# Scores of a windowed attention: keys and queries split into two float16 and multiplied on the two halves of the rows, in place of float32r keys stacked for each head

## The chip, the cores and the metric

The kernel runs on one core of a Trainium2 chip. The metric is the device time of one execution in microseconds, as a median of three runs. A profile of one execution gives the instructions of each engine: TensorE (PE, its weight loads as PEld), VectorE (DVE), ScalarE (ACT), GpSimd (POOL) and the DMA queue issued from SyncE (SP).

## The reference

Attention with four batches, eight heads, 768 positions and a head dimension of 64. Each position sees the first `n_sink` = 4 keys and the last `window` = 128 keys. The result (3072 tokens of width 512) goes through a feed-forward layer of width 2048 with an ELU between.

```python
scores = np.matmul(q, k.transpose(0, 1, 3, 2)) / np.sqrt(64)
rel = pos[:, None] - pos[None, :]
keep = (pos[None, :] < n_sink) | ((rel >= 0) & (rel < window))
a = softmax(np.where(keep, scores, -1e9))
x = np.matmul(a, v)                       # heads side by side: 3072 x 512
h = x @ w_in                              # 512 x 2048
g = np.where(h > 0, h, np.exp(np.minimum(h, 0)) - 1)
out = g @ w_out                           # 2048 x 512
```

Inputs are float32 and the output is float32. Precision beyond float16 is had by splitting a number into a float16 `hi` and a float16 rest `lo` and adding products: hi·hi + lo·hi + hi·lo.

## The kernel before

The 24 tiles of 128 tokens are grouped into nine chunks (`SIZES`: three of 2 tiles, six of 3). For a chunk, `attention(c)` goes over four pairs of heads and, in each pair, over the tiles. `feed_forward` then goes over the 16 slices of the hidden width (`NF`): twelve matmuls into `h` (L671), the ELU (L679 to L682), its split (`gh` on ACT, L684, and `gl` on POOL, L685), and 6 or 9 matmuls into `acc` (L692). The first two chunks take the feed-forward in two halves (`PARTS`), while the weights arrive: each of the 32 weight pieces comes as 64-bit words, is turned into float32 on ACT and DVE (L287 to L290), and is split into two float16 (ACT L436, POOL L437).

Attention of a tile and a pair of heads: scores for both heads into two banks `s`; mask and row minimum on DVE (L586), exponential on ACT (L588), normalised and split into float16 (ACT L600, DVE L601), transposed by a DMA (L619), multiplied with the split values on the two halves of the columns (`po`, L630 and L635), and moved out as `x` (L643, L644). A tile has keys of two tiles (264 columns with the sinks, `nb` = 2), or of one where it is the first tile of a batch (132 columns, `nb` = 1).

How the scores are made differs by chunk. In the first two chunks (`c < WHOLE`) the raw float32 keys and queries of a pair lie on the two halves of the 128 rows, 64 rows a head, and L567 multiplies them in float32. From the third chunk on (`c >= DUP`) each head has a block of its own, with its keys on both halves of the rows. `split_keys` loads it (L502), rounds keys and queries to float32r on ACT (L503), takes the rest of the keys on POOL (L507) and writes the rest of the queries over the lower half of the queries (L509, 64 rows). So one pass over 128 rows gives hi·hi + lo·hi: L560 multiplies by the keys' `hi`, L561 by their `lo`. These are two matmuls a head and four a pair, each with a float32r operand.

The order of work is written out ahead of time by a planner (`Plan`): tasks with modelled durations, a PE order by `pos`, list scheduling by due time on the other engines, and rings of buffers (`kq` = 3, `kqs` = 2, `s` = 2) as dependences. `keep_order` then fixes that order on each engine. At the end, `in_range` (L743) checks on DVE that sums, values and weights were within the limits of the split; its result decides whether `general_path` (a slow path, not run for these inputs) follows.

Of the kernel before, what the change touches and what calls it, by code (L numbers as in the profile page):

```python
# [9 lines left out]
F32 = mybir.dt.float32  # L10
# [35 lines left out]
LAG = 2  # L46
ROUNDS = 8
WHOLE = 2
DUP = 2
AHEAD = 5  # L50
V_AT = 7
V_AT0 = 5.0
# [3 lines left out]
def key_tiles(ch):  # L56

    return sorted({g for g in ch} | {g - 1 for g in ch if g % NT})
# [5 lines left out]
for _c, _ch in enumerate(CHUNKS):  # L64
    for _p in range(NP):
        V_OFF[_c, _p] = V_COLS
        V_COLS += (len(key_tiles(_ch)) + 1) * P
        for _e in range(2):
            KQ_OFF[_c, 2 * _p + _e] = KQ_COLS
            if _c >= DUP or _e:  # L70
                KQ_COLS += len(key_tiles(_ch)) * KW + len(_ch) * P
KQ_MAX = max(len(key_tiles(c)) * KW + len(c) * P for c in CHUNKS)
KL_MAX = max(len(key_tiles(c)) * KW for c in CHUNKS)
NK_MAX = max(len(key_tiles(c)) for c in CHUNKS)
TOK_MAX = max(SIZES) * P

# [267 lines left out]
def fast_path(tc, ctx, first, kq, vx, wt, out, nw, flag):  # L344
# [11 lines left out]

    kqs = first["kqs"]
    vs = first["vs"]
    kqr = rows("kq", [P, KQ_MAX + KL_MAX], F32R)
    vh = rows("vh", [P, (NK_MAX + 1) * P], F16, RINGS["vhl"])  # L360
    vl = rows("vl", [P, (NK_MAX + 1) * P], F16, RINGS["vhl"])
    vm = rows("vm", [P, NP, TOK_MAX], F32)
# [34 lines left out]

    nc1, nc2 = len(SIZES) * NF, len(SIZES) * NP  # L400
    checks = pool.tile([P, nc1 + nc2 + NW], F32, name="checks")
    es_of, v_top, w_top = checks[:, :nc1], checks[:, nc1 : nc1 + nc2], checks[:, nc1 + nc2 :]
    some = pool.tile([P, 4], F32, name="some")[:, 0:3]
    some16 = pool.tile([P, 4], BF16, name="some16")[:, 0:3]

# [66 lines left out]
    def attention(c):  # L472
# [14 lines left out]
        def split_keys(h):  # L487


            st = kqs[slot("kqs")]  # L490
            buf = kqr[slot("kq")] if c >= WHOLE else None
            o, kw = KQ_OFF[c, h], kc + qc
            if c < WHOLE:
                ld = None
                if (c, h) not in first["kq"]:
                    ld = add("SP", 0.4, lambda: nc.sync.dma_start(st[:, :kw], kq[:, o : o + kw]), lat=dma_us(P * kw * 4))
                users = []
                return st, None, ld, ld, users
            raw, hi = st[:, :kw], buf[:, :kw]
            ld = None  # L500
            if (c, h) not in first["kq"]:
                ld = add("SP", 0.4, lambda: nc.sync.dma_start(raw, kq[:, o : o + kw]), lat=dma_us(P * kw * 4))  # L502
            th = add("ACT", act_us(kw), lambda: nc.scalar.activation(hi, raw, AF.Copy), deps=[ld])  # L503

            def low():
                n = kc if c >= DUP else kw
                nc.gpsimd.tensor_tensor(buf[:, KQ_MAX : KQ_MAX + n] if c >= DUP else buf[:, kw : 2 * kw], raw[:, :n], hi[:, :n].bitcast(F32), ALU.subtract)  # L507
                if c >= DUP:
                    nc.gpsimd.tensor_tensor(hi[D:, kc:], raw[D:, kc:], hi[D:, kc:].bitcast(F32), ALU.subtract)  # L509

            tl = add("POOL", pool_us(kc) + pool_us(qc) if c >= DUP else pool_us(kw), low, deps=[th])
            users = []
            ring("kqs", [ld or th], [th, tl])
            ring("kq", [th], users)
            lo = buf[:, KQ_MAX : KQ_MAX + kc] if c >= DUP else buf[:, kw : 2 * kw]
            return hi, lo, th, tl, users

        k = 0
        for p in range(NP):
            kqp = [split_keys(2 * p + e) for e in range(2 if c >= DUP else 1)]  # L520


            st = vs[slot("vs")]
# [17 lines left out]
            for g in ts:  # L541
# [10 lines left out]
                pq = pqs[slot("pq")]  # L552
                pt = pts[slot("pt")]

                def scores(es_, sps=sps, qo=qo, c0=c0, wd=wd, kqp=kqp):
                    def run():
                        if c >= DUP:
                            hi, lo = kqp[es_[0]][:2]
                            sp, q = sps[es_[0]], hi[:, qo : qo + P]
                            nc.tensor.matmul(sp[:, :wd], q, hi[:, c0 : c0 + wd], start=True, stop=False)  # L560
                            nc.tensor.matmul(sp[:, :wd], q, lo[:, c0 : c0 + wd], start=False, stop=True)  # L561
                            return
                        hi, lo = kqp[0][:2]
                        if c < WHOLE:
                            for e in es_:
                                r = slice(e * D, (e + 1) * D)
                                nc.tensor.matmul(sps[e][:, :wd], hi[r, qo : qo + P], hi[r, c0 : c0 + wd], start=True, stop=True)  # L567
                            return
                        for n, (a, b) in enumerate(((hi, hi), (lo, hi), (hi, lo))):
                            for e in es_:  # L570
                                r = slice(e * D, (e + 1) * D)
                                nc.tensor.matmul(sps[e][:, :wd], a[r, qo : qo + P], b[r, c0 : c0 + wd], start=n == 0, stop=n == 2)
                    return run

                if c >= DUP:
                    scs = [add("PE", 0.22 if nb == 2 else 0.45, scores([e]), deps=kqp[e][2:4], pos=at[k] + 0.01 * e, line=1) for e in range(2)]
                else:
                    scs = [add("PE", 0.75, scores([0, 1]), deps=kqp[0][2:4], pos=at[k], line=1)] * 2
                for kk, sc_ in zip(kqp, scs):
                    kk[4].append(sc_)  # L580
                if c < WHOLE and j == 0:
                    ring("kqs", [kqp[0][2] or scs[0]], kqp[0][4])
                exps, st_users = [], []
                for e in range(2):
                    ee, me = e3[:, e, :wd], mn[:, e : e + 1]
# [155 lines left out]
        seen += new  # L741

    def in_range():  # L743
        for r, most in ((es_of, EXP_MAX), (v_top, V_MAX)):
            nc.vector.tensor_scalar(r, r, most, None, ALU.is_le)
        for i in range(2):
            nc.vector.tensor_reduce(some[:, 1 + i : 2 + i], w_top[:, i::2], AX.X, ALU.max)
        nc.vector.tensor_scalar(w_top, w_top, W_MAX, None, ALU.is_le)
        nc.vector.tensor_reduce(some[:, 0:1], checks, AX.X, ALU.min)
        nc.vector.tensor_scalar(some[:, 1:3], some[:, 1:3], W_MIN, float(P), ALU.is_ge, ALU.mult)  # L750
        nc.vector.tensor_copy(some16, some)
# [5 lines left out]
        nc.vector.tensor_tensor(flag, flag, some[:, 0:1], ALU.mult)  # L757

    sp = s_ps[slot("s")]
    a = add("DVE", 2.0, in_range, deps=seen + exps_done)  # L760
    b = add("PE", 0.1, lambda: nc.tensor.matmul(sp[:, 0:3], ones, some16, start=True, stop=True), deps=[a], pos=start + 2 * LAG - 1.5)
    ring("s", [b], [add("DVE", 0.6, decide, deps=[b])])
    for writer, users in later:
# [27 lines left out]
def general_path(tc, ctx, kq, vx, wt, out, nw):  # L791
# [50 lines left out]
    for b in range(B):  # L842
        x = sb.tile([P, ND, S], F32, name=f"g_x{b}", tag="g_x", bufs=1)
        for h in range(H):
# [3 lines left out]
            for c, ch in enumerate(CHUNKS):  # L848
                kts = key_tiles(ch)
                for i, g in enumerate(ch):  # L850
                    if g // NT != b:
                        continue
                    j, ts = kts.index(g), slice(g % NT * P, (g % NT + 1) * P)
                    o = KQ_OFF[c, h]
                    r = slice(0, D) if c >= DUP else slice(h % 2 * D, (h % 2 + 1) * D)
                    nc.sync.dma_start(kt[:, ts], kq[r, o + j * KW + NS : o + (j + 1) * KW])
                    o += len(kts) * KW + i * P
                    nc.sync.dma_start(qt[:, ts], kq[r, o : o + P])
                    o = V_OFF[c, h // 2] + j * P + (h % 2) * D
                    nc.sync.dma_start(vt[:, g % NT, :], vx[:, o : o + D])  # L860
# [47 lines left out]
def layouts(q, k, v):  # L908

    kT = k.transpose(0, 1, 3, 2).reshape(B, H, D, NT, P)
    kx = np.concatenate([np.broadcast_to(kT[:, :, :, :1, :NS], (B, H, D, NT, NS)), kT], axis=4)
    qT = q.transpose(0, 1, 3, 2).reshape(B, H, D, NT, P)
    kq = np.empty((P, KQ_COLS), q.dtype)
    vx = np.zeros((P, V_COLS), v.dtype)
    for c, ch in enumerate(CHUNKS):
        kts = key_tiles(ch)  # L920
        far = [g // NT for g in ch if g % NT >= 2]
        for h in range(H):
            e = h % 2
            o = KQ_OFF[c, h]
            for src, tiles in ((kx, kts), (qT, ch)):
                for g in tiles:
                    w = src.shape[4]
                    for r in (0, 1) if c >= DUP else (e,):
                        kq[r * D : (r + 1) * D, o : o + w] = src[g // NT, h, :, g % NT]
                    o += w  # L930
            o = V_OFF[c, h // 2] + e * D
            for g in kts:
                vx[:, o : o + D] = v[g // NT, h, g % NT * P : (g % NT + 1) * P]
                o += P
            if far:
                assert min(far) == max(far)
                for r in range(e * NS, 96, 32):
                    vx[r : r + NS, o : o + D] = v[far[0], h, :NS]
    return kq, vx
# [77 lines left out]
```

## Time and profile before

| | |
|---|---|
| median of 3 runs | 658.06 us (657.52 to 658.17) |
| the profiled execution | 658.03 us, its span 656.2 us (1.8 us lie around the span) |
| granted TensorE clock, mean | 0.984 |
| PE / PEld busy | 611.0 us (93%) / 370.1 us (56%) |
| DVE / ACT / POOL busy | 458.4 / 456.3 / 338.8 us |
| chain that ended last | PE 81%, DVE 8%, DMA 3%, ACT 2%, POOL 2% |

The busy time of an engine is how long it had an instruction under way; of PE's matmuls the ends are modelled and neighbours overlap, so a matmul's price is read from the distance of two starts, not from its duration. The chain is followed back from the last instruction to whatever released each step.

### The profile page before, as it was taken

The numbers are of one execution on the slowest core, as the hardware profiler recorded it, in microseconds if no ns is written. First come the engines' busy times: TensorE is split into PE (matmuls) and PEld (weight loads), VectorE is DVE, ScalarE is ACT, GpSimd is POOL, SyncE is SP. The second block draws the span as 40 slices with busy tenths as digits, with TensorE's granted clock in tenths as the row PEclk, the third lists the DMA queues.
The fourth block names the chain that finished last, engine by engine and source line by source line (L and its number), as shares of the span: only waits on it lengthen the run. The fifth ranks groups of instructions, "written<-read, shape, count | busy, mean of one in ns | idle before, by whom it ended". The sixth has DMA issues, their size and how long they took to land.

```text
span 656.2 us, 13438 instructions
## 1 busy us (share of the span) xinstructions
PE 611.0 (93%) x4449; PEld 370.1 (56%) x4449; DVE 458.4 (70%) x1251; ACT 456.3 (70%) x1340; POOL 338.8 (52%) x497
## 2 busy tenths in 40 slices
PE   3678699789999999999999999999999999999995
PEld 2444466457777665655555565565555556555552
DVE  6999999987677757757676877757686786533222
ACT  4988798887788878767677877766677776523221
POOL 0156878785565767544446656544446654212221
PEclk9998699999999999999999999999999999999998
DMA  7898976765647556445454666454655733211001
GB/s 266 202 284 231 267 213 209 246 171 154 140 126 155 159 151 129 117 116 158 100 147 114 186 135 164 79 157 136 125 140 122 213 91 90 61 42 44 1 0 54
DMA packets 130110, 93.41 MB, mean 142 GB/s; under 512 B 104432, under 2 KB 109552, under 8 KB 130032
## 3 DMA queue, kind: packets, MB, share of 16 engines
q1 hardware_dynamic: 130032, 92.47, 53.2%
q8 instruction: 37, 0.61, 0.4%
q14 instruction: 41, 0.34, 0.2%
HBM read 59.94 MB, written 7.34 MB: 103 GB/s over the span
## 4 chain that ended last, share of the span: by engine, by line
PE 81%; DVE 8%; DMA 3%; ACT 2%; issue 2%; POOL 2%; SPq 0%; DVEq 0%; POOLq 0%; ACTq 0%
PE h L671 35%; PE acc L692 34%; PE po L630 5%; PE s L560 3%; PE s L561 3%; DMA pt<-pq 2%; DVE wv L290 2%; DVE wu L288 1%; DVE pq L601 1%; PE s L567 1%; DVE wu L289 1%; DVE g L681 1%; POOL w L437 1%; ACT e L588 1%; ACT pq L600 1%
## 5 line engine op out<-in xcount | busy, mean ns | idle before, releaser
L671 PE MATMUL h<-x,w 128*128 128x384 f16 (+1 forms) x1728 | 278.1, 312 | 6.1 <-DVE g L682 6.1
L685 POOL TENSOR_TENSOR gl<-g,gh 128x384 f16<-128x384 f32 (+1 forms) x144 | 125.7, 874 | 195.8 <-ACT gh L684 163.2
L671 PEld LDWEIGHTS <-w 128*128 128x128 f16 x1728 | 166.5, 99 | 100.6 <-POOL w L437 4.0
L692 PE MATMUL acc<-w,gh 128*128 128x512 f16 x768 | 194.2, 382 | 0.7 <-ACT gh L684 0.7
L681 DVE TENSOR_SCALAR g<-g 128x384 f32<-128x384 f32 (+1 forms) x144 | 68.2, 474 | 109.1 <-ACT g L679 108.8
L679 ACT ACTIVATE g<-h 128x384 f32<-128x384 f32 (+1 forms) x144 | 65.0, 451 | 84.6 <-PE h L671 77.3
L601 DVE SCALAR_TENSOR_TENSOR pq<-e,st,pq 128x256 f16<-128x256 f32 (+1 forms) x192 | 104.7, 573 | 15.1 <-ACT pq L600 14.5
L692 PE MATMUL acc<-w,gl 128*128 128x512 f16 x384 | 109.3, 380 | 2.4 <-POOL gl L685 2.3
L692 PEld LDWEIGHTS <-gh 128*128 128x128 f16 x768 | 70.0, 98 | 70.9 <-ACT gh L684 1.2
L586 DVE CUSTOM_DVE_ANT_0 e<-s,m 128x264 f32<-128x264 f32 (+1 forms) x192 | 73.5, 404 | 41.5 <-PE s L561 38.0
L588 ACT ACTIVATE e<-e,st 128x264 f32<-128x264 f32 (+1 forms) x192 | 93.4, 487 | 11.5 <-DVE st L586 10.1
L684 ACT ACTIVATE gh<-g 128x384 f16<-128x384 f32 (+1 forms) x144 | 69.2, 481 | 44.6 <-DVE g L682 44.1
L600 ACT ACTIVATE pq<-e,st 128x256 f16<-128x256 f32 (+1 forms) x192 | 84.6, 479 | 10.0 <-DVE st L593 9.4
L507 POOL TENSOR_TENSOR kq<-kqs,kq 128x396 fp32r<-128x396 f32 (+1 forms) x56 | 68.5, 1224 | 37.8 <-ACT kq L503 37.2
L682 DVE SCALAR_TENSOR_TENSOR g<-g,h 128x384 f32<-128x384 f32 (+1 forms) x144 | 72.5, 503 | 1.3
L692 PEld LDWEIGHTS <-gl 128*128 128x128 f16 x384 | 37.5, 98 | 49.0 <-POOL gl L685 4.1
L503 ACT ACTIVATE kq<-kqs 128x780 fp32r<-128x780 f32 (+2 forms) x56 | 48.5, 878 | 17.1 <-PE s L561 15.5
L509 POOL TENSOR_TENSOR kq<-kqs,kq 64x384 fp32r<-64x384 f32 (+1 forms) x56 | 57.0, 1017 | 4.4
L560 PE MATMUL s<-kq 128*128 128x264 f32 x160 | 56.0, 367 | 3.0 <-DVE st L586 2.1
L437 POOL TENSOR_TENSOR w<-wv,w 128x512 f16<-128x512 f32 x32 | 38.8, 1218 | 37.2 <-DVE wu L289 16.6
L630 PE MATMUL po<-pt,vh 128*64 128x128 f16 x704 | 42.1, 230 | 7.7 <-DVE x L644 5.0
L561 PE MATMUL s<-kq 128*128 128x264 f32 x160 | 42.8, 284 | 0.0
(78 smaller groups left out, 620.7 us busy)
## 6 DMA issues: line engine op xcount, KB each, us to landing
raw<-in_wt_dram SPq DMA_DIRECT2D x32, 512.0 KB, 5.2
kqs<-in_kq_dram SPq DMA_DIRECT2D x24, 456.0 KB, 3.4
kqs<-in_kq_dram SPq DMA_DIRECT2D x24, 390.0 KB, 3.3
out_dram<-wv SPq DMA_DIRECT2D x24, 256.0 KB, 2.4
vs<-in_vx_dram SPq DMA_DIRECT2D x20, 256.0 KB, 2.8
vm<-in_vx_dram SPq DMA_DIRECT2D x6, 768.0 KB, 4.8
kqs<-in_kq_dram SPq DMA_DIRECT2D x12, 326.0 KB, 3.4
vs<-in_vx_dram SPq DMA_DIRECT2D x12, 320.0 KB, 3.1
```

The lines of the kernel that those rows point to most:

```text
L560: nc.tensor.matmul(sp[:, :wd], q, hi[:, c0 : c0 + wd], start=True, stop=False)
L586: red = add("DVE", 0.13 + 0.00145 * wd, lambda ee=ee, me=me, sp=sps[e], m=m, wd=wd: nc.vector.tensor_tensor_reduce(ee, sp[:, :wd], m[:, :w ...
L588: ex = add("ACT", 0.48 + 0.00085 * wd, lambda ee=ee, me=me, rs=rs[:, e : e + 1]: nc.scalar.activation(ee, ee, AF.Exp, bias=me, scale=-1.0, ...
L600: a = add("ACT", act_us(nb * P, True), lambda src=src, hi=hi, re=re: nc.scalar.activation(hi, src, AF.Copy, scale=re), deps=[rr])
L601: b = add("DVE", dve_us(nb * P) + 0.1, lambda src=src, hi=hi, lo=lo, re=re: nc.vector.scalar_tensor_tensor(lo, src, re, hi, ALU.mult, ALU. ...
L630: nc.tensor.matmul(po[e * D : (e + 1) * D, oc], vv[:, vo : vo + D], pt[:, (2 * e + part) * nb + i, :], start=new, stop=last)
L671: nc.tensor.matmul(hp[:, :n], win[:, part, d, :], xx[:, :n], start=k == 0, stop=k == 3 * ND - 1)
L681: b = add("DVE", 0.1 + 0.0008 * n, lambda gf=gf: nc.vector.tensor_scalar(gf, gf, -1.0, G_SCALE, ALU.add, ALU.mult), deps=[a])
L682: b = add("DVE", dve_us(n), lambda gf=gf, hp=hp: nc.vector.scalar_tensor_tensor(gf, gf, 0.0, hp[:, :n], ALU.min, ALU.max), deps=[b])
L684: th = add("ACT", act_us(n), lambda gf=gf, gh=gh: nc.scalar.activation(gh[:, :n], gf, AF.Copy), deps=[b])
L685: tl = add("POOL", pool_us(n), lambda gl=gl, gf=gf, gh=gh: nc.gpsimd.tensor_tensor(gl[:, :n], gf, gh[:, :n], ALU.subtract), deps=[th])
L692: nc.tensor.matmul(acc[i], gg[:, i * P : (i + 1) * P], wout[:, part, :], start=f == f0 and k == 0, stop=f == f1 - 1 and k == 2)
```

## The change

From the third chunk on, the keys and queries of a pair of heads now come as one block of 128 rows, 64 rows a head, as in the first two chunks. ACT rounds the block to float16, POOL subtracts to get a float16 rest of the whole block, and a new reduction on DVE takes the largest magnitude of the rounded block into `kq_top`, which `in_range` compares with 16 at the end. The scores of a pair are three products a head, hi·hi, lo·hi and hi·lo, over 64 rows each, the two heads on the two halves of the rows and alternating: six matmuls. They are one PE task for both heads where there was one task a head. The layout of the input in memory loses the second copy of each head, `general_path` reads it accordingly, and the planner's durations for the scores change.

```diff
-DUP = 2
+KQ_TOP = 16.0
...
-            if _c >= DUP or _e:
+            if _e:
                 KQ_COLS += len(key_tiles(_ch)) * KW + len(_ch) * P
...
-    kqr = rows("kq", [P, KQ_MAX + KL_MAX], F32R)
+    kqr = rows("kq", [P, 2, KQ_MAX], F16)
...
-    nc1, nc2 = len(SIZES) * NF, len(SIZES) * NP
-    checks = pool.tile([P, nc1 + nc2 + NW], F32, name="checks")
+    nc1, nc2, nc3 = len(SIZES) * NF, len(SIZES) * NP, (len(SIZES) - WHOLE) * NP
+    checks = pool.tile([P, nc1 + nc2 + NW + nc3], F32, name="checks")
+    kq_seen = []
...
-            raw, hi = st[:, :kw], buf[:, :kw]
+            raw, hi, lo = st[:, :kw], buf[:, 0, :kw], buf[:, 1, :kw]
...
             th = add("ACT", act_us(kw), lambda: nc.scalar.activation(hi, raw, AF.Copy), deps=[ld])
-
-            def low():
-                n = kc if c >= DUP else kw
-                nc.gpsimd.tensor_tensor(buf[:, KQ_MAX : KQ_MAX + n] if c >= DUP else buf[:, kw : 2 * kw], raw[:, :n], hi[:, :n].bitcast(F32), ALU.subtract)
-                if c >= DUP:
-                    nc.gpsimd.tensor_tensor(hi[D:, kc:], raw[D:, kc:], hi[D:, kc:].bitcast(F32), ALU.subtract)
-
-            tl = add("POOL", pool_us(kc) + pool_us(qc) if c >= DUP else pool_us(kw), low, deps=[th])
-            users = []
+            tl = add("POOL", pool_us(kw), lambda: nc.gpsimd.tensor_tensor(lo, raw, hi, ALU.subtract), deps=[th])
+            at_ = len(kq_seen)
+            tm = add("DVE", 0.12 + 0.00108 * kw, lambda: nc.vector.tensor_reduce(kq_top[:, at_ : at_ + 1], hi, AX.X, ALU.max, apply_absolute_value=True), deps=[th])
+            kq_seen.append(tm)
+            users = [tm]
             ring("kqs", [ld or th], [th, tl])
             ring("kq", [th], users)
...
-            kqp = [split_keys(2 * p + e) for e in range(2 if c >= DUP else 1)]
+            kqp = split_keys(2 * p)
...
+                def scores(sps=sps, qo=qo, c0=c0, wd=wd, kqp=kqp):
+                    hi, lo = kqp[:2]
+                    products = ((hi, hi),) if c < WHOLE else ((hi, hi), (lo, hi), (hi, lo))
+                    for n, (a, b) in enumerate(products):
+                        for e in range(2):
+                            r = slice(e * D, (e + 1) * D)
+                            nc.tensor.matmul(sps[e][:, :wd], a[r, qo : qo + P], b[r, c0 : c0 + wd], start=n == 0, stop=n == len(products) - 1)
...
-                if c >= DUP:
-                    scs = [add("PE", 0.22 if nb == 2 else 0.45, scores([e]), deps=kqp[e][2:4], pos=at[k] + 0.01 * e, line=1) for e in range(2)]
-                else:
-                    scs = [add("PE", 0.75, scores([0, 1]), deps=kqp[0][2:4], pos=at[k], line=1)] * 2
+                scs = [add("PE", 0.75 if c < WHOLE else 0.4 if nb == 2 else 0.25, scores, deps=kqp[2:4], pos=at[k], line=1)] * 2
+                kqp[4].append(scs[0])
...
-        for r, most in ((es_of, EXP_MAX), (v_top, V_MAX)):
+        for r, most in ((es_of, EXP_MAX), (v_top, V_MAX), (kq_top, KQ_TOP)):
...
-    a = add("DVE", 2.0, in_range, deps=seen + exps_done)
+    a = add("DVE", 2.0, in_range, deps=seen + exps_done + kq_seen)
...
-                    r = slice(0, D) if c >= DUP else slice(h % 2 * D, (h % 2 + 1) * D)
+                    r = slice(h % 2 * D, (h % 2 + 1) * D)
...
-                    for r in (0, 1) if c >= DUP else (e,):
-                        kq[r * D : (r + 1) * D, o : o + w] = src[g // NT, h, :, g % NT]
+                    kq[e * D : (e + 1) * D, o : o + w] = src[g // NT, h, :, g % NT]
```

## Rows read from the trace of the kernel before

**Rows 1.** Busy time of each engine in four stretches of the span, with the number of instructions, the granted TensorE clock, the share of the DMA engines and their GB/s.

```profile
60.00:97.00 37.00, 27.82 (x232) 19.06 (x232) 35.36 (x81) 31.84 (x86) 30.29 (x44) 0.86 0.87 235
97.00:144.00 47.00, 41.03 (x320) 27.23 (x319) 46.85 (x102) 39.26 (x106) 37.91 (x48) 1.00 0.66 210
144.00:220.00 76.00, 75.08 (x658) 52.97 (x657) 51.63 (x166) 60.83 (x203) 46.71 (x66) 1.00 0.60 145
220.00:570.00 350.00, 350.00 (x2553) 206.33 (x2552) 248.42 (x673) 255.72 (x741) 186.79 (x281) 1.00 0.52 132
```

**Rows 2.** The chain that ended last, its shares by line: first of the stretch from 97 to 144 us, then of that from 220 to 580 us.

```profile
by line: DVE wv L290 17.5%; DVE wu L288 15.7%; DVE wu L289 13.5%; DVE g L681 12.6%; DVE pq L601 9.4%; issue 8.7%; DVE g L682 6.8%; DVE e L586 4.3%; PE h L671 3.8%; POOL kq L509 2.8%; PE s L560 1.4%; ACT kq L503 1.4%; ACT g L679 1.0%; DVE st
...
by line: PE h L671 43.1%; PE acc L692 42.9%; PE po L630 5.8%; PE s L561 3.7%; PE s L560 3.7%; PE po L635 0.7%
```

**Rows 3.** The matmuls of a score block in order of time: start and length in us, then line, output and inputs, sizes and count. The first four rows are the third and fourth matmul of a block of 264 columns at 301 us with the matmuls before and after the block; the last two are what stands before and after a block of 132 columns at 312 us.

```profile
300.18 0.98 PE L671 MATMUL h<-x,w 128*128 128x384 f16 x5
...
301.24 0.28 PE L560 MATMUL s<-kq 128*128 128x264 f32 x1
301.36 0.28 PE L561 MATMUL s<-kq 128*128 128x264 f32 x1
301.49 0.60 PE L692 MATMUL acc<-w,gh 128*128 128x512 f16 x2
...
312.19 0.81 PE L692 MATMUL acc<-w,gl 128*128 128x512 f16 x3
...
313.24 0.34 PE L671 MATMUL h<-x,w 128*128 128x384 f16 x1
```

**Rows 4.** Two pieces of the chain in order of time: start, length on the chain, and what; nine `acc` matmuls and twelve `h` matmuls.

```profile
301.64 1.96 PE acc L692 x9
303.60 1.95 PE h L671 x12
```

**Rows 5.** All first score matmuls of a head (L560) from 145 to 575 us, in two forms: count, busy us, mean ns, idle time of PE before them.

```profile
L560 PE MATMUL s<-kq 128*128 128x264 f32 x120 | 41.9, 369 | 0.0
L560 PE MATMUL s<-kq 128*128 128x132 f32 x24 | 7.9, 346 | 0.9 <-POOL kq L509 0.9
```

**Rows 6.** Matmuls in order of time where the float32 scores of the second chunk use the two halves of the rows (64 rows each). The first two rows are the last values matmuls ahead of the block and the first products of both heads; the last two are the second products of both heads and the `h` matmul behind.

```profile
55.98 0.22 PE L635 MATMUL po<-pt,vh 128*64 128x128 f16 x2
56.13 0.49 PE L567 MATMUL s<-kqs 64*128 64x264 f32 x2
...
56.46 0.39 PE L567 MATMUL s<-kqs 64*128 64x264 f32 x2
56.78 0.28 PE L671 MATMUL h<-x,w 128*128 128x256 f16 x1
```

**Rows 7.** Matmuls in order of time where the values use the two halves of the columns: the entry at 305 us and the exit at 306 us.

```profile
304.90 0.65 PE L671 MATMUL h<-x,w 128*128 128x384 f16 x3
305.48 0.25 PE L630 MATMUL po<-pt,vh 128*64 128x128 f16 x2
305.56 0.22 PE L630 MATMUL po<-pt,vl 128*64 128x128 f16 x2
...
306.23 0.28 PE L630 MATMUL po<-pt,vh 128*64 128x128 f16 x4
306.34 0.22 PE L635 MATMUL po<-pt,vh 128*64 128x128 f16 x2
306.50 0.61 PE L692 MATMUL acc<-w,gh 128*128 128x512 f16 x2
```

**Rows 8.** DVE and POOL instructions from 60 to 144 us by line and form: count, busy us, mean ns.

```profile
L288 DVE TENSOR_SCALAR wu<-raw 128x512 uint16<-128x512 uint16 x21 | 17.1, 816 | 0.0
L289 DVE TENSOR_SCALAR wu<-raw 128x512 uint16<-128x512 uint16 x20 | 14.2, 711 | 0.0
L681 DVE TENSOR_SCALAR g<-g 128x256 f32<-128x256 f32 x22 | 13.1, 597 | 0.2 <-ACT g L679 0.2
...
L507 POOL TENSOR_TENSOR kq<-kqs,kq 128x396 fp32r<-128x396 f32 x9 | 10.4, 1156 | 2.3 <-ACT kq L503 2.3
L509 POOL TENSOR_TENSOR kq<-kqs,kq 64x256 fp32r<-64x256 f32 x8 | 7.3, 915 | 0.6
```

**Rows 9.** Three DVE lines over the whole span: count, then the shortest, median and longest duration in ns, and the time of the first and last start.

```profile
L288 DVE TENSOR_SCALAR wu<-raw x32: 433/730/1409, 13.8 to 135.3; 128x512 uint16<-128x512 uint16 x32
L289 DVE TENSOR_SCALAR wu<-raw x32: 433/452/1428, 12.4 to 134.2; 128x512 uint16<-128x512 uint16 x32
L681 DVE TENSOR_SCALAR g<-g x144: 266/360/1241, 37.9 to 643.4; 128x384 f32<-128x384 f32 x96, 128x256 f32<-128x256 f32 x48
```

**Rows 10.** Instructions over the whole span by line and form that are near the added and removed ones: count, busy us, mean ns.

```profile
L507 POOL TENSOR_TENSOR kq<-kqs,kq 128x528 fp32r<-128x528 f32 x24 | 32.8, 1366 | 20.8 <-ACT kq L503 20.6
...
L732 DVE TENSOR_REDUCE checks<-w 128x1 f32<-128x512 f16 x32 | 21.6, 676 | 0.0
...
L739 DVE TENSOR_REDUCE checks<-vm 128x1 f32<-128x256 f32 x12 | 4.4, 405 | 0.0
```

**Rows 11.** The last microseconds in order of time on DVE, ACT and PE's weight loads: start, length, line, and in brackets how long the engine had been idle and what ended it.

```profile
643.64 0.32 DVE L745 TENSOR_SCALAR checks<-checks 128x144 f32<-128x144 f32 x2
...
645.50 0.52 ACT L684 ACTIVATE gh<-g 128x384 f16<-128x384 f32 x1 [2.17 <-DVE g L682]
...
647.12 0.10 PEld L692 LDWEIGHTS <-gl 128*128 128x128 f16 x1 [0.62 <-POOL gl L685]
```

More of the change, by code (lines that the diff above doesn't have):

```diff
@@ L69 @@
             KQ_OFF[_c, 2 * _p + _e] = KQ_COLS
-            if _c >= DUP or _e:
+            if _e:
                 KQ_COLS += len(key_tiles(_ch)) * KW + len(_ch) * P
 KQ_MAX = max(len(key_tiles(c)) * KW + len(c) * P for c in CHUNKS)
-KL_MAX = max(len(key_tiles(c)) * KW for c in CHUNKS)
 NK_MAX = max(len(key_tiles(c)) for c in CHUNKS)
@@ L396, in fast_path @@
     rest_ = add("DVE", 0.9, rest)
-    nc1, nc2 = len(SIZES) * NF, len(SIZES) * NP
-    checks = pool.tile([P, nc1 + nc2 + NW], F32, name="checks")
-    es_of, v_top, w_top = checks[:, :nc1], checks[:, nc1 : nc1 + nc2], checks[:, nc1 + nc2 :]
+    nc1, nc2, nc3 = len(SIZES) * NF, len(SIZES) * NP, (len(SIZES) - WHOLE) * NP
+    checks = pool.tile([P, nc1 + nc2 + NW + nc3], F32, name="checks")
+    es_of, v_top, w_top, kq_top = checks[:, :nc1], checks[:, nc1 : nc1 + nc2], checks[:, nc1 + nc2 : nc1 + nc2 + NW], checks[:, nc1 + nc2 + NW :]
+    kq_seen = []
     some = pool.tile([P, 4], F32, name="some")[:, 0:3]
@@ L503, in split_keys @@
             th = add("ACT", act_us(kw), lambda: nc.scalar.activation(hi, raw, AF.Copy), deps=[ld])
-            def low():
-                n = kc if c >= DUP else kw
-                nc.gpsimd.tensor_tensor(buf[:, KQ_MAX : KQ_MAX + n] if c >= DUP else buf[:, kw : 2 * kw], raw[:, :n], hi[:, :n].bitcast(F32), ALU.subtract)
-                if c >= DUP:
-                    nc.gpsimd.tensor_tensor(hi[D:, kc:], raw[D:, kc:], hi[D:, kc:].bitcast(F32), ALU.subtract)
-            tl = add("POOL", pool_us(kc) + pool_us(qc) if c >= DUP else pool_us(kw), low, deps=[th])
-            users = []
+            tl = add("POOL", pool_us(kw), lambda: nc.gpsimd.tensor_tensor(lo, raw, hi, ALU.subtract), deps=[th])
[3 more added lines that the diff above has]
+            users = [tm]
             ring("kqs", [ld or th], [th, tl])
             ring("kq", [th], users)
-            lo = buf[:, KQ_MAX : KQ_MAX + kc] if c >= DUP else buf[:, kw : 2 * kw]
             return hi, lo, th, tl, users
@@ L553, in attention @@
                 pt = pts[slot("pt")]
-                def scores(es_, sps=sps, qo=qo, c0=c0, wd=wd, kqp=kqp):
-                    def run():
-                        if c >= DUP:
[L558 to L573, printed above, removed]
@@ L575, in attention @@
-                if c >= DUP:
-                    scs = [add("PE", 0.22 if nb == 2 else 0.45, scores([e]), deps=kqp[e][2:4], pos=at[k] + 0.01 * e, line=1) for e in range(2)]
-                else:
-                    scs = [add("PE", 0.75, scores([0, 1]), deps=kqp[0][2:4], pos=at[k], line=1)] * 2
-                for kk, sc_ in zip(kqp, scs):
-                    kk[4].append(sc_)
+                def scores(sps=sps, qo=qo, c0=c0, wd=wd, kqp=kqp):
[5 more added lines that the diff above has]
+                            nc.tensor.matmul(sps[e][:, :wd], a[r, qo : qo + P], b[r, c0 : c0 + wd], start=n == 0, stop=n == len(products) - 1)
@@ L581, in attention @@
+                scs = [add("PE", 0.75 if c < WHOLE else 0.4 if nb == 2 else 0.25, scores, deps=kqp[2:4], pos=at[k], line=1)] * 2
+                kqp[4].append(scs[0])
                 if c < WHOLE and j == 0:
-                    ring("kqs", [kqp[0][2] or scs[0]], kqp[0][4])
+                    ring("kqs", [kqp[2] or scs[0]], kqp[4])
                 exps, st_users = [], []
```

## The prediction

> **What bounds the kernel now.** I read the busy times by stage first [rows 1]. They show two regimes. From 60 to 144 us DVE is busy 82.2 of 84 us (35.36 + 46.85), while PE has 15 us without work. From 144 us on PE is busy 75.08 of 76 us and then 350 of 350 us, at a granted clock of 1.00, the 2.4 GHz level. The chain of waits says the same [rows 2]: from 97 to 144 us its largest shares are the weight conversion on DVE (L288 to L290) and the ELU's first DVE step (L681); from 220 to 580 us all of it is PE. So in the second regime what counts is how long PE's stream is, and nothing else. In the first it is how much DVE has to do until the last weights are converted, and what holds DVE up.
>
> Most of the changed work is in the second regime: of the first score matmuls, 120 of 264 columns and 24 of 132 lie there [rows 5], two to a block, so 60 wide and 12 narrow blocks. Only the third chunk's eight blocks come before 144 us, where PE has room.
>
> **The price of a score block before.** A busy PE says nothing of a price, so I go by distances of starts. A matmul of 384 columns takes 1.95/12 = 0.163 us of the stream and one of 512 takes 1.96/9 = 0.218 us [rows 4]; by the column that is 0.000423 us. The five `h` matmuls that begin at 300.18 leave the stream free at 300.99, and `acc` begins at 301.49: the wide block costs 0.50 us, of which each of the four matmuls takes 0.12 [rows 3]. So it has next to nothing at its edges. The narrow block lies between 312.19 + 3 x 0.218 = 312.84 and 313.24: 0.40 us [rows 3].
>
> **The price of a score block after.** No float16 matmul on 64 rows is in the trace; it is put together from its nearest rows.
> - Do the two heads overlap? The float32 scores of the second chunk use the same two halves of the rows [rows 6]. Both heads' first products start at 56.13 and both second ones at 56.46, and the `h` matmul follows at 56.78. A float32 product streams 264 columns twice, 528 x 0.000423 = 0.22 us. Four in a row would be 0.89 us, yet all lies within 0.65. So the halves do overlap, and I price six matmuls as three: 3 x 264 x 0.000423 = 0.335 us wide, 0.168 narrow.
> - Entering and leaving. The values matmul ahead leaves the stream at 55.98 + 0.055 = 56.035 (0.055 is half of the 0.11 between 306.23 and 306.34, where four values matmuls run as two pairs [rows 7]); the halves begin at 56.13, a hole of 0.095. The second float32 products end at 56.46 + 0.22 = 56.68, and `h` begins at 56.78: 0.10 [rows 6]. The values matmuls, on halves of the columns, have the same: in at 304.90 + 3 x 0.163 = 305.39 to 305.48, out at 306.395 to 306.50 [rows 7]. I take 0.095 in and 0.10 out.
> - The first weight load, which nothing covers behind such a hole: 0.10 for float32 (0.49 against 0.39 for the next [rows 6]), 0.03 for float16 with 64 columns (0.25 against 0.22 [rows 7]). I take 0.025, with 0 and 0.10 as the ends.
>
> Wide: 0.095 + 0.025 + 0.335 + 0.10 = 0.555 us against 0.50, so +0.055 to +0.06; narrow: 0.388 against 0.40, so -0.01. Over the regime: 60 x 0.06 - 12 x 0.01 = **+3.5 us**. With the load hidden it is +1.7; with 0.10 exposed, +8.9.
>
> **The work off PE.** After 144 us all of this is covered by PE's stream: half the roundings on ACT (60.83 of 76 us and 255.72 of 350 busy), half the loads of keys and their issues on SP (DMA share 0.60 and 0.52), far less on POOL, and on DVE, with 51.63 of 76 and 248.42 of 350 us, 24 reductions of about 1 us [rows 1]. If PE's cover were gone these reductions would cost 24 us. The other layout in memory and `general_path` execute nothing here.
>
> Before 144 us it does count, in both directions.
> - Added on DVE: the reductions of the third chunk. 256 elements take 0.405 us and 512 take 0.676 [rows 10], so 652 elements take 0.676 + 140 x 0.00106 = 0.82 us; four make **+3.3 us**. A reduction is wanted only when its buffer is taken again three splits later, so two could be put off past 144 us (+1.65); five, with one of the next chunk (780 elements, 0.96), make +4.3. Queued behind each on DVE are the weight conversion and the ELU, for which POOL and PE wait.
> - Removed on POOL: eight heads at 1.156 + 0.915 us [rows 8], 16.6 us, become four splits of 652 elements. By 1156 ns for 396 [rows 8] and 1366 for 528 [rows 10] that is 1.56 us each, 6.2 in all: 10.4 us less of POOL's 68.2 [rows 1].
> - What that gives DVE: L288, L289 and L681 take 816, 711 and 597 ns on average there [rows 8], and 433, 433 and 266 at their shortest [rows 9]. The excess is 21 x 0.383 + 20 x 0.278 + 22 x 0.331 = 20.9 us. I put it down to POOL's instructions under way at the time, 20.9/68.2 = 0.31 us for each us of POOL, so 10.4 us less of them give **-3.2 us** (ends: 0, and -5.1 if the keys' share of POOL's time, 16.6/68.2, goes altogether).
>
> Sum of the first regime: +0.1 us.
>
> The Trainium skill (GPSIMD Engine Reference, "Specifications") says that GpSimd's SBUF interfaces are shared with VectorE, and that DVE instructions in a two-port mode or with two SBUF inputs contend. The long and short L681 of rows 9 agree with it. By that rule the new reductions, with one input, wait for nobody, and the sum stays +0.1.
>
> **The tail.** `in_range` stands between L681 and L682 of the last slice; ACT waits 2.17 us for L682 there, and PE behind it 0.62 us for `gl` [rows 11]. One more comparison (0.16, half of the 0.32) and a wider reduction (28 x 0.00106 = 0.03): **+0.2 us**.
>
> **Sum.** The profiled execution took 658.03 us, 0.03 from the median of the runs: 658.03 + 3.5 + 0.1 + 0.2 = **661.8 us**.
>
> **The rivals.** What this kernel's measurement can tell from no change is about 0.2%, 1.3 us.
> - A, the forecast: holes at the edges eat more than the shorter stream saves; 658 to 666. Chance 0.50.
> - B, faster by POOL's relief: the first regime ends early. At its bounds: stalls -5.1, two reductions put off, so +1.65, and DVE's own 1.8 us of idle time closed [rows 1]; -5.2 + 3.5 + 0.2 gives 656.5, and 655 with the load hidden. It decides from 5 us gained there. For it: DVE is the limit there and POOL holds it up. Against: DVE gets new work in the same place. 0.17.
> - C, no holes: float16 halves follow `h` as the full rows do. Wide 0.36, narrow 0.19: 60 x -0.14 - 12 x 0.21 = -10.9, so 647.4. Against: rows 6 and 7 show holes for halves of the rows in float32 and halves of the columns in float16. 0.08.
> - D, the halves don't overlap in float16: wide 0.22 + 6 x 0.112 = 0.89, narrow 0.22 + 6 x 0.056 = 0.56; 60 x 0.39 + 12 x 0.16 = +25.3, so 683.6. Then the change doesn't do what it says. Against: the overlap of rows 6 and 7. 0.06.
> - E, the reductions come at full price and the relief doesn't: +4.3 in the first regime, 666.0. For it: L288 can meet the weights' own POOL work as well. 0.19.
>
> Of C the Trainium skill has both sides (TensorEngine Tiling): "Theoretical Speedup" gives up to 2x for a contraction of at most 64, by which alone the wide block would be three streams of 0.112 and the time C's 647; "Key Properties" says that a change of the tiling mode drains the engine. The trace agrees with the second: 0.095 in, 0.10 out.
>
> **How the numbers follow.** The time is A's sum, 661.8. The range reaches down to B at its bound, 655.5, and up to E with a little more of the load exposed, 667; it leaves out C, D and the ends of the load. Faster than 656.7: C and most of B, 0.21. Within 0.2%: the rest of B and the low edge of A (load hidden, +1.7 on PE, and some gain early), 0.16. Slower: 0.63.
>
> **What would show it.** Right: a score block whose first matmul starts 0.09 us after the stream ahead is free, pairs of starts a few ns apart with 0.11 us from pair to pair, 0.10 us behind the last; 0.55 us wide and 0.39 narrow; PE still busy throughout from some 144 us on. L681 and L288 shorter on average before 144 us, DVE as full as now. Wrong: starts of the two heads 0.11 us apart (D), no hole ahead (C), PE's unbroken stretch beginning more than 4 us earlier (B) or later (E), or holes in PE after 150 us, which none of these cases has.

## The result and the profile after

The changed kernel took 663.15 us (661.93 to 665.32, five runs) against 657.60 for the kernel before, a ratio of 1.0086 (95% interval 1.0061 to 1.0110). It is slower, inside the range and on the forecast side; the point forecast was 661.8, and the execution profiled took 661.93 (span 660.0).

Busy time by stage, with the columns of [rows 1]:

```profile
60.00:97.00 37.00, 26.81 (x229) 16.45 (x228) 33.80 (x80) 30.84 (x89) 23.80 (x36) 0.94 0.86 247
97.00:144.00 47.00, 39.59 (x314) 24.96 (x311) 45.86 (x93) 35.69 (x98) 32.43 (x39) 1.00 0.54 169
144.00:220.00 76.00, 75.82 (x702) 48.04 (x702) 63.52 (x190) 60.12 (x207) 34.56 (x55) 1.00 0.59 137
220.00:570.00 350.00, 349.92 (x2657) 182.34 (x2656) 251.32 (x684) 238.61 (x713) 136.36 (x221) 1.00 0.48 107
```

PE is still full from 144 us on. DVE, which was forecast to stay as full as before, has become less full ahead of that: 79.7 of 84 us (33.80 + 45.86), where it was 82.2.

A wide block (264 columns) and a narrow one (132) with their neighbours, in order of time (the answers to [rows 3]):

```profile
302.35 0.98 PE L650 MATMUL h<-x,w 128*128 128x384 f16 x5
303.26 0.51 PE L556 MATMUL s<-kq 64*128 64x264 f16 x6
303.70 0.61 PE L671 MATMUL acc<-w,gh 128*128 128x512 f16 x2
...
314.46 0.81 PE L671 MATMUL acc<-w,gl 128*128 128x512 f16 x3
315.20 0.35 PE L556 MATMUL s<-kq 64*128 64x132 f16 x6
315.48 0.34 PE L650 MATMUL h<-x,w 128*128 128x384 f16 x1
```

The `h` matmuls leave the stream at 302.35 + 5 x 0.163 = 303.165; the block begins 0.095 us later, and `acc` comes at 303.70: 0.535 us, against 0.50. The narrow block lies between 315.11 and 315.48: 0.37, against 0.40.

DVE and POOL from 60 to 144 us (the answers to [rows 8]), and all the new reductions with their shortest, median and longest duration and the time of the first and last:

```profile
L288 DVE TENSOR_SCALAR wu<-raw 128x512 uint16<-128x512 uint16 x21 | 15.3, 729 | 0.0
L287 DVE TENSOR_SCALAR wu<-raw 128x512 uint16<-128x512 uint16 x21 | 15.1, 719 | 0.0
L660 DVE TENSOR_SCALAR g<-g 128x256 f32<-128x256 f32 x21 | 12.7, 606 | 1.4 <-ACT g L658 1.4
...
L504 POOL TENSOR_TENSOR kq<-kqs,kq 128x652 f16<-128x652 f32 x4 | 6.3, 1568 | 0.9 <-DVE wu L287 0.5 <-ACT kq L503 0.5
...
L506 DVE TENSOR_REDUCE checks<-kq x28: 816/962/1105, 137.6 to 514.2; 128x1 f32<-128x780 f16 x12, 128x1 f32<-128x912 f16 x12, 128x1 f32<-128x652 f16 x4
```

The planner put every reduction off to 137.6 us or later.

Two marks in every trace tell the two regimes apart: the start of the `h` slice that opens the feed-forward of the fourth chunk, when PE is already full, and that of the last `h` matmul.

| kernel | fourth chunk's first `h`, us | last `h` matmul, us | between |
|---|---|---|---|
| before | 218.46 | 642.3 | 423.8 |
| after | 220.56 | 646.1 | 425.5 |
| after_again | 223.06 | 648.6 | 425.5 |
| tiny_reduce | 221.92 | 647.5 | 425.6 |
| small_pool_rest | 214.14 | 637.9 | 423.8 |
| halves_old_order | 216.54 | 642.6 | 426.1 |
| planner_real_prices | 216.40 | 642.5 | 426.1 |
| head_by_head | 225.18 | 651.1 | 425.9 |
| before_lower_prices | 222.05 | 646.2 | 424.2 |
| full_rows_f16 | 216.20 | 635.9 | 419.7 |
| full_rows_checked | 214.37 | 634.9 | 420.5 |
| full_rows_real_prices | 217.14 | 637.9 | 420.8 |

The first column of times holds what happens early (some blocks of the third and fourth chunks too), the last one the price of the remaining blocks. What lies behind the last mark is within a microsecond or so the same. Each row is one execution, and the two of the changed kernel lie 2.5 us apart at the first mark; so for the early part the medians of the runs count more than one mark.

### The profile page after: what moved, and what is told of

Same layout as the page of the kernel before. It is cut to its first block, busy times and chain, and to the rows that moved or that the text cites. A ratio compares the mean times of both kernels' runs of the same rounds, so it can differ in the third digit from the quotient of the medians.

```text
span 660.0 us, 13501 instructions
## 1 busy us (share of the span) xinstructions
PE 611.3 (93%) x4609; PEld 337.7 (51%) x4609; DVE 471.9 (71%) x1280; ACT 435.1 (66%) x1312; POOL 264.7 (40%) x413
## 4 chain that ended last, share of the span: by engine, by line
PE 75%; DVE 3%; issue 1%; POOL 1%; ACT 0%; DVEq 0%; ACTq 0%; POOLq 0%
PE h L650 33%; PE acc L671 33%; PE s L556 5%; PE po L609 4%; DVE wv L289 1%; DVE wu L287 0%; PE po L614 0%; DVE pq L580 0%; POOL w L437 0%; DVE g L660 0%; DVE g L661 0%; DVE wu L288 0%; DVE e L565 0%; DVE wv L692 0%; DVE checks L506 0%
## 5 line engine op out<-in xcount | busy, mean ns | idle before, releaser
L650 PE MATMUL h<-x,w 128*128 128x384 f16 (+1 forms) x1728 | 278.0, 311 | 14.6 <-POOL w L437 8.5
L664 POOL TENSOR_TENSOR gl<-g,gh 128x384 f16<-128x384 f32 (+1 forms) x144 | 129.2, 897 | 250.2 <-ACT gh L663 209.5
L650 PEld LDWEIGHTS <-w 128*128 128x128 f16 x1728 | 165.6, 98 | 116.4 <-POOL w L437 12.0
L660 DVE TENSOR_SCALAR g<-g 128x384 f32<-128x384 f32 (+1 forms) x144 | 62.0, 431 | 95.3 <-ACT g L658 95.1
L580 DVE SCALAR_TENSOR_TENSOR pq<-e,st,pq 128x256 f16<-128x256 f32 (+1 forms) x192 | 100.8, 556 | 14.5 <-ACT pq L579 13.6
L504 POOL TENSOR_TENSOR kq<-kqs,kq 128x780 f16<-128x780 f32 (+2 forms) x28 | 49.8, 1779 | 25.2 <-ACT kq L503 21.1
L437 POOL TENSOR_TENSOR w<-wv,w 128x512 f16<-128x512 f32 x32 | 39.1, 1226 | 48.2 <-ACT w L436 31.2
L556 PE MATMUL s<-kq 64*128 64x264 f16 (+1 forms) x480 | 40.0, 267 | 2.8 <-DVE st L565 2.5
L609 PEld LDWEIGHTS <-vh 128*64 128x64 f16 x704 | 30.2, 113 | 23.6 <-issue 21.5
L586 POOL TENSOR_TENSOR st<-e,st 128x8 f32<-128x8 f32 x64 | 16.5, 258 | 53.0 <-DVE st L572 53.0
L567 ACT ACTIVATION_READ_ACCUMULATOR e<-e,st 128x1 f32 x192 | 36.2, 188 | 0.0
```

The costliest lines, as they stand in the source:

```text
L567: ex = add("ACT", 0.48 + 0.00085 * wd, lambda ee=ee, me=me, rs=rs[:, e : e + 1]: nc.scalar.activation(ee, ee, AF.Exp, bias=me, scale=-1.0, ...
L580: b = add("DVE", dve_us(nb * P) + 0.1, lambda src=src, hi=hi, lo=lo, re=re: nc.vector.scalar_tensor_tensor(lo, src, re, hi, ALU.mult, ALU. ...
L609: nc.tensor.matmul(po[e * D : (e + 1) * D, oc], vv[:, vo : vo + D], pt[:, (2 * e + part) * nb + i, :], start=new, stop=last)
L650: nc.tensor.matmul(hp[:, :n], win[:, part, d, :], xx[:, :n], start=k == 0, stop=k == 3 * ND - 1)
L664: tl = add("POOL", pool_us(n), lambda gl=gl, gf=gf, gh=gh: nc.gpsimd.tensor_tensor(gl[:, :n], gf, gh[:, :n], ALU.subtract), deps=[th])
```

## The experiments

The first four ran on one chip, beside the kernel before at 657.73 us. In the cuts of code `...` stands for what is left out.

**after_again**: the changed kernel, unedited.

> The changed kernel once more, for its spread and a second profile. Theory 1 (the blocks): in any execution the stretch from 220 to 580 us is the same, a wide score block 0.54 us and a narrow one 0.375, and all that differs from run to run lies before 150 us. Time 662 to 664, the ratio to the kernel before 1.006 to 1.011. Rival (the slow stretch is anywhere): the spread lies in PE's unbroken stretch too.

663.93 us, ratio 1.0095 (1.0076 to 1.0115). The second profile is 2.4 us longer than the first; at the first mark it is already 2.5 us late, and between the marks both take 425.5. So what these two executions differ by lies early, where the granted clock of the second is also lower (0.82 against 0.94; the higher level is 1.00). Whether the clock makes the difference isn't shown.

```profile
60.00:97.00 37.00, 29.48 (x224) 17.53 (x223) 33.85 (x80) 30.00 (x84) 23.26 (x35) 0.82 0.85 243
```

Theory 1's part on the spread holds for these two.

**tiny_reduce**: the new reductions over 4 columns.

```diff
-... nc.vector.tensor_reduce(kq_top[:, at_ : at_ + 1], hi, AX.X, ALU.max, apply_absolute_value=True)
+... nc.vector.tensor_reduce(kq_top[:, at_ : at_ + 1], hi[:, :4], AX.X, ALU.max, apply_absolute_value=True)
```

> The changed kernel with each of the 28 new reductions cut to 4 columns; order of all engines and planner as in the changed kernel. It leaves out the range check of the other columns. Theory 1 (PE's stream alone decides after 144 us, and the reductions were put off past 137 us): nothing comes back beyond one reduction, 0 to 0.8 us less than the changed kernel, about 662.5. Rival (the reductions delay something that PE waits for): up to 3.3 us less, near 660.

663.59 us, ratio 1.0095 (1.0074 to 1.0115), as the unedited one. The length of the reductions costs nothing that can be told; the 28 instructions themselves stay, at 0.15 us each.

**small_pool_rest**: POOL's second subtraction in the kernel before, over 4 columns.

```diff
-nc.gpsimd.tensor_tensor(hi[D:, kc:], raw[D:, kc:], hi[D:, kc:].bitcast(F32), ALU.subtract)
+nc.gpsimd.tensor_tensor(hi[D:, kc : kc + 4], raw[D:, kc : kc + 4], hi[D:, kc : kc + 4].bitcast(F32), ALU.subtract)
```

> The kernel before with POOL's second subtraction of each head (the rest of the queries, 64 rows) cut to 4 columns; the order is that of the kernel before. It leaves out the rest of the queries in all but 4 columns. 8 x 0.8 = 6.5 us of POOL's work before 144 us are gone. Step of the prediction (0.31 us of DVE stall for each us of POOL): 2.0 us less than before, 655.6. Rival (DVE meets other POOL work instead, as the changed kernel's trace suggests with 0.13 for each us): 0.8 us or less, no difference that can be told.

654.32 us, ratio 0.996 (0.9942 to 0.9978): 2.6 us faster by the ratio, 3.4 by the medians. The gain is there and lies early (214.14 at the first mark), with nothing between the marks. Less POOL work was gone than I had put down, since an instruction of 4 columns still takes 0.395 us, so 8 x 0.52 = 4.2 us:

```profile
L509 POOL TENSOR_TENSOR kq<-kqs,kq 64x4 fp32r<-64x4 f32 x10 | 3.9, 395 | 0.8
```

DVE's instructions did get shorter with it: L288, L289 and L681 take 719, 716 and 582 ns on average from 60 to 144 us, an excess of 18.3 us by the working of the prediction, where it was 20.9. That is 2.6 us less, as much as the kernel gained. The step is right in kind and rather low in size.

**full_rows_f16**: the kernel before with float16 in place of float32r.

```diff
-    kqr = rows("kq", [P, KQ_MAX + KL_MAX], F32R)
+    kqr = rows("kq", [P, KQ_MAX + KL_MAX], F16)
...
-... raw[:, :n], hi[:, :n].bitcast(F32), ALU.subtract)
+... raw[:, :n], hi[:, :n], ALU.subtract)
```

> The kernel before with float16 in place of float32r for the split keys and queries, still stacked for each head over 128 rows: two products a head, no halves of the array, no new reductions; the planner's order is that of the kernel before. It leaves out a check that float16 holds the keys' and queries' range. Theory 1 (what costs is the two holes at a block's edges): without holes a wide block is 4 x 0.112 + 0.02 = 0.465 against 0.50 before, a narrow one 4 x 0.056 + 0.02 = 0.245 against 0.40, so 60 x 0.03 + 12 x 0.155 = 3.7 us less than before, about 654. Rival (float16 score matmuls cost as such, or weight loads pace them): as the kernel before, 657.6, or slower.

650.61 us, ratio 0.9893 (0.9872 to 0.9914): 7.1 us less, where 3.7 were expected. Its blocks:

```profile
297.22 0.65 PE L671 MATMUL h<-x,w 128*128 128x384 f16 x3
297.70 0.28 PE L560 MATMUL s<-kq 128*128 128x264 f16 x1
297.82 0.28 PE L561 MATMUL s<-kq 128*128 128x264 f16 x1
297.93 0.28 PE L560 MATMUL s<-kq 128*128 128x264 f16 x1
298.04 0.28 PE L561 MATMUL s<-kq 128*128 128x264 f16 x1
298.15 0.59 PE L692 MATMUL acc<-w,gh 128*128 128x512 f16 x2
...
308.81 0.81 PE L692 MATMUL acc<-w,gl 128*128 128x512 f16 x3
309.45 0.22 PE L560 MATMUL s<-kq 128*128 128x132 f16 x1
...
309.68 0.49 PE L671 MATMUL h<-x,w 128*128 128x384 f16 x2
```

The stream is free at 297.71 and `acc` comes at 298.15: 0.44 to 0.45 us, four streams with no hole at all; the narrow block takes 0.22 to 0.23. So the changed kernel streams less in a wide block (three times 0.112 in place of four) and is still slower by 0.09, which is what its two holes cost beyond the stream saved. Between the marks this kernel saves 4.1 us, about what was expected; the rest of its gain is early, and what makes it is not shown.

The next four ran beside the kernel before at 657.88 us.

**halves_old_order**: the changed kernel's work without reductions, in the order of the kernel before.

```diff
+            own = h % 2 == 0
...
-            th = add("ACT", act_us(kw), lambda: nc.scalar.activation(hi, raw, AF.Copy), deps=[ld])
+            th = add("ACT", act_us(kw), lambda: own and (gen.__setitem__(slot_, (c, h)), nc.scalar.activation(hi, raw, AF.Copy)), deps=[ld])
...
+            tl = add("POOL", pool_us(kc) + pool_us(qc), lambda: own and nc.gpsimd.tensor_tensor(lo, raw, hi, ALU.subtract), deps=[th])
...
+                        if c >= DUP and (es_[0] == 0 or once):
+                            return
+                        once.append(1)
+                        if c >= DUP:
+                            es_ = [0, 1]
```

> The changed kernel's work (pairs in one block of 128 rows, float16, six matmuls on the two halves of the rows) without the reductions, issued in the order of the kernel before: the planner sees the tasks and durations of the kernel before, the second head's split tasks issue nothing, and the pair's six matmuls stand where the second head's two stood. It leaves out the range check of keys and queries. Theory 2 (the changed kernel loses its first microseconds to the new order alone): PE's stretch from 220 to 580 us is as long as the changed kernel's, but the stretch before 150 us ends 2 to 4 us earlier than the kernel before's, as with the small POOL rest; time 656 to 659. Rival (pairing itself costs in the beginning, whatever the order): 661.5 to 664, as the changed kernel.

657.92 us, ratio 1.0000 (0.9982 to 1.0017). Between the marks it is as slow as the changed kernel (426.1), and at the first mark 1.9 us ahead of the kernel before. Its first regime, and below it three of DVE's lines from 60 to 144 us:

```profile
60.00:97.00 37.00, 28.23 (x257) 18.19 (x257) 32.08 (x83) 30.83 (x85) 25.00 (x37) 0.91 0.84 230
97.00:144.00 47.00, 40.19 (x333) 25.10 (x331) 45.64 (x102) 39.03 (x112) 34.63 (x43) 1.00 0.62 188
...
L288 DVE TENSOR_SCALAR wu<-raw 128x512 uint16<-128x512 uint16 x21 | 15.1, 717 | 0.0
...
L289 DVE TENSOR_SCALAR wu<-raw 128x512 uint16<-128x512 uint16 x20 | 14.0, 700 | 0.2 <-DMA raw<-in_wt_dram 0.2
...
L684 DVE TENSOR_SCALAR g<-g 128x256 f32<-128x256 f32 x22 | 10.9, 494 | 0.3
```

DVE is busy 77.7 us where it was 82.2, with about as many instructions (185 against 183). So in the old order the holes and POOL's relief cancel, and pairing as such costs nothing early.

**planner_real_prices**: the changed kernel, complete, with another pair of durations in the planner.

```diff
-... 0.75 if c < WHOLE else 0.4 if nb == 2 else 0.25 ...
+... 0.75 if c < WHOLE else 0.54 if nb == 2 else 0.375 ...
```

> The changed kernel with the planner's durations of a score block set to the measured 0.54 and 0.375 us in place of 0.40 and 0.25; nothing else. Theory 2 (the order in the first 150 us is what costs there): the stretch before 150 us moves by some us either way, the blocks stay at 0.54 and 0.375; 660 to 665. Rival (the planner's prices make no odds): 663.5 to 664, with the same trace.

658.42 us, ratio 0.9999 (0.9978 to 1.0019): 5.5 us less than the changed kernel in after_again, with the same instructions (the ratios differ by 0.0096, 6.3 us). Between the marks nothing changed in its favour (426.1 against 425.5); at the first mark it is 4.2 and 6.7 us ahead of the two profiles of the changed kernel. The move is larger than theory 2 had expected, and the rival falls.

**head_by_head**: the products of one head, then those of the other.

```diff
-                    for n, (a, b) in enumerate(products):
-                        for e in range(2):
+                    for e in range(2):
+                        for n, (a, b) in enumerate(products):
```

> The changed kernel with the six matmuls of a block in another order: three products of the first head, then three of the second. Theory 1 (the two halves run at once only where neighbours in the queue are of different halves): 5 or 6 streams in place of 3, a wide block 0.76 to 0.88 in place of 0.54 and a narrow one 0.49 to 0.55 in place of 0.375, so 14 to 23 us more than the changed kernel, 678 to 687. Rival (TensorE finds the overlap itself): 663.5, as the changed kernel.

665.33 us, ratio 1.0109 (1.0076 to 1.0141), so my expectation fell:

```profile
263.86 0.81 PE L671 MATMUL acc<-w,gl 128*128 128x512 f16 x3
264.61 0.52 PE L556 MATMUL s<-kq 64*128 64x264 f16 x6
265.06 0.34 PE L650 MATMUL h<-x,w 128*128 128x384 f16 x1
```

The block still takes 265.06 - 264.51 = 0.55 us. Less the two holes (0.195) that is 0.35 us, room for three streams of 0.112 and not for five or six. So the two heads ran side by side; TensorE found the overlap although three products of one head stood first. Between the marks the kernel is 0.4 us longer than the changed one; the rest of what it is slower by lies early.

**full_rows_checked**: the float16 full-row kernel with the range check, from loads of its own.

```diff
+    for k, (c, p) in enumerate((c, p) for c in range(DUP, len(SIZES)) for p in range(NP)):
...
+                nc.sync.dma_start(t[r, :kw], kq[r, o : o + kw])
...
+        ld = add("SP", 0.8, load, deps=[exps_done[NF * 4 + 2 * k]], lat=dma_us(P * kw * 4))
+        tm = add("DVE", 0.12 + 0.00108 * kw, lambda t=t, kw=kw, k=k: nc.vector.tensor_reduce(kq_top[:, k : k + 1], t[:, :kw], AX.X, ALU.max, apply_absolute_value=True), deps=[ld])
```

> The kernel with float16 over full rows and the missing range check added: from 300 us on the keys and queries are loaded once more, as the values are, 28 loads of one pair each, and 28 reductions on DVE take their largest magnitudes. Theory 1 (after 150 us nothing but PE's stream counts): the loads and 28 us of DVE's time cost nothing, 650 to 652, beyond 0.2 us in the tail. Rival (they hold up what PE waits for): up to 28 us of DVE come through, over 655.

650.42 us, ratio 0.9896 (0.9869 to 0.9923), as full_rows_f16: the check is free there, and this complete kernel is faster than the kernel before and the changed one.

The last two ran beside the kernel before at 658.20 us.

**before_lower_prices**: the kernel before with other durations in the planner.

```diff
-... 0.22 if nb == 2 else 0.45 ...
+... 0.2 if nb == 2 else 0.125 ...
```

> The kernel before with the planner's durations of a head's scores set to half of what the changed kernel gives a pair: 0.20 and 0.125 us in place of 0.22 and 0.45. Not one instruction differs but in order. Theory 2 (the planned order alone moves the first 150 us by microseconds): the stretch from 220 us on is the same, the one before it is not: 1.5 us or more away from the kernel before, on the later side if prices that are too low do the harm. Rival (the order does not matter, and the changed kernel lost its time to its new tasks): 657.9, within 1 us.

660.66 us, ratio 1.0036 (1.0022 to 1.0050): 2.4 us slower from order alone; in the profiles it is nearly all ahead of the first mark (222.05 against 218.46; 424.2 against 423.8 between the marks).

**full_rows_real_prices**: full_rows_checked with 0.225 and 0.115 in that place.

> The kernel with float16 over full rows and the late range check, with the planner's durations of a head's scores set to the measured ones, 0.225 and 0.115 us, in place of 0.22 and 0.45. Theory 2: PE's stretch stays as it is, the beginning moves by up to 3 us either way: 648 to 653. Rival (no effect of the order): 650.4, within 1 us.

652.91 us, ratio 0.9908 (0.9893 to 0.9923). The median is 2.5 us above that with the old prices, which was taken on another chip; but the two ratios, 0.9908 and 0.9896, differ by 0.8 us, well within their intervals. So real prices are not better ones here, and whether they are worse can't be told.

## Why the prediction was right, and where its steps were off

- **The blocks.** Right in each part: the halves overlap, 0.095 us of hole ahead, about 0.10 behind. The whole was 0.02 us too high for both widths (0.535 and 0.37 against 0.555 and 0.388), since the first weight load shows only some 0.01. By the prediction's sum these prices give 60 x 0.035 - 12 x 0.03 = +1.7; between the marks it is +1.7 to +2.3 us; +3.5 was forecast.
- **The reductions** (+3.3): mis-sized. I let all four come before 144 us; the trace has the first at 137.6 and no other before 144, and tiny_reduce gives nothing back.
- **POOL's relief** (-3.2): there in the old order. By the working of the prediction DVE's excess falls there to 16.3 us from 20.9 (L288 717, L289 700 and the ELU step 494 ns on average), and small_pool_rest is 2.6 us faster. With the other durations (planner_real_prices) it even falls to 13.0 (668, 611, 480). In the changed kernel's first profile only 1.6 of it is seen (719, 729, 606: only the first of the three lines became shorter), in its second nothing. So the relief depends on the order too.
- **What the sum lacked: the new order.** Tasks and durations in the planner changed, so all engines got another order in the first 150 us. planner_real_prices puts that at about 5.5 us for the same instructions, and halves_old_order lies 6.0 us under after_again. The steps came to +3.8 us and 5.55 were measured (663.15 - 657.60): the number came out by luck, because this missing term stood in for the two that were too large. In the old order the sum comes to nothing (halves_old_order, 657.92).
- **The tail** (+0.2): not seen; from the last `h` matmul on, both profiles take 13.9 us.
- Rival B was right that POOL's relief ends the first regime earlier, but not that this outweighs the holes: with another order the two cancel (657.92 and 658.42). C and D fell with the first block shown; E's reductions at full price fell with tiny_reduce, though the relief did fail to come in the changed kernel's order, as E had it.

The traces narrow down where the order costs. Here are POOL's weight splits (L437) and the `h` matmuls (L650), each with the idle time before them that ended with the weights (us, times; for `h`, PE and its weight loads together), first in the changed kernel and then in planner_real_prices:

```profile
L437 POOL TENSOR_TENSOR w<-wv,w x32: 1153/1162/1602, 18.7 to 142.9; 128x512 f16<-128x512 f32 x32
  ACT w L436: 31.2, 19
L650 PE MATMUL h<-x,w x1728: 269/326/421, 38.9 to 646.1; 128*128 128x384 f16 x128, 128*128 128x256 f16 x64
  POOL w L437: 20.5, 15
...
L437 POOL TENSOR_TENSOR w<-wv,w x32: 1153/1160/1460, 18.7 to 140.0; 128x512 f16<-128x512 f32 x32
  ACT w L436: 10.9, 15
L650 PE MATMUL h<-x,w x1728: 269/326/421, 34.1 to 642.5; 128*128 128x384 f16 x128, 128*128 128x256 f16 x64
  POOL w L437: 2.6, 2
```

In the changed kernel's order ACT rounds weights later (the fourth piece at 39.70 us in place of 34.44, behind an attention step that waits 2.17 us for PE), POOL waits longer for it, the first `h` matmul begins 4.8 us later, and PE waits more for splits of weights. So it is in all four traces of that order (first `h` at 38.9 to 39.3 us, also in after_again, tiny_reduce and head_by_head) and in none of the others (34.1 to 35.8). The granted clock does not explain it: from 60 to 97 us it was 0.94 in the changed kernel's first profile and 0.86 in planner_real_prices. Which single turn of the order makes the weights late was not tested, and before_lower_prices loses its 2.4 us without it (first `h` at 34.7).

## What to carry to other kernels

Price a form of matmul by the whole block, from the last stream before to the first one after: halves of the array paid 0.2 us a visit here, and float16 over full rows, with more streaming, beat the kernel before by 1% and the changed one by 2%. Where a planner sets the order, a change of its durations is a change of its own; undo it, or run the old order, before a difference of about 1% is put down to the instructions.

## What the hardware showed unexpectedly

TensorE paired the halves by itself in head_by_head: with three products of one head ahead of three of the other, the wide block took 0.55 us against 0.535 when they alternate. And float32r matmuls of 132 columns took 0.10 us each in a block (0.40/4, [rows 3]), where float16 ones of the same width took 0.06 (full_rows_f16), although at 264 columns they differ by a tenth only (0.12 and 0.11). Why the narrow float32r ones cost so much is open.
